# A fused retention and wave-MLP kernel: a new written-out order of its steps, with 39 DMA transposes instead of 35, and output tiles that share the token weights' buffers

## The chip, the core and the metric

The kernel runs on one core of a Trainium2 chip. The metric is the device time of one execution in microseconds; the kernel before has a median of 168.93 us over 11 runs (167.72 to 171.47). Profiles are of single executions.

## What is computed

For 4 batches, 8 heads, 768 tokens and a head width of 64, the state of each head decays by gamma and takes up k times v, and q reads it out:

```python
for t in range(S):
    state = gamma * state + outer(k[t], v[t])      # per batch and head
    y[t] = scale * q[t] @ state
```

The heads' results side by side give x with 512 columns. Then for each batch, with five products of matrices:

```python
theta = x @ w_theta
y = w_tok_r @ (x * cos(theta)) + w_tok_i @ (x * sin(theta))   # over tokens, 768 x 768
u = x + y
out = u + maximum(u @ w_ch, 0)
```

## The kernel before, in words

Both stages are cut into blocks, and the blocks of both are mixed. The retention is cut into 24 *units* n: a batch, a third of its tokens (256) and half of its heads. The MLP is cut into 24 *chunks* C of 128 tokens, six to a batch, and 24 output *tiles* t of 128 tokens, also six to a batch.

For a unit: Lk, Lq and Lv load k, q and v (0.262 MB each). ck, cq and cv cast them to bf16 and scale q and v; the letter after the second point names the engine (p POOL, v DVE, a ACT). k and q have to be transposed: either Tk and Tq do so on PE (4 matmuls each) and E copies the result out of PSUM, or Dk (line 309) does both with one DMA transpose from SBUF to SBUF, issued on SP. G runs three steps on PE: A of this unit (16 matmuls, scores), Y of the unit before (16, scores times v) and ST of this unit (16, the state's increment). m masks the scores on DVE, SU adds up the state on DVE, SB copies it as bf16, I reads the state out with q (2 or 4 matmuls), XA copies the result as xT on ACT.

For a chunk: Hh makes theta (4 matmuls of 512 columns), CN takes sine and cosine on ACT. x itself is xT transposed back, by Tx on PE and a copy Ex, or by Dx (line 434), a DMA transpose on SP. z multiplies x with sine and cosine.

The weights: Lth and Lch load w_theta and w_ch (1.049 MB each), cth and cch cast them. Lw loads a row block of a token weight (0.393 MB; the tile `wtok`, 4 buffers), cw casts it, Tw transposes it on PE (6 matmuls), Ew copies it out.

For a tile: M.t.0 to M.t.5 sum over the six chunks of the batch (2 matmuls of 512 columns each), u adds x on DVE, then u is transposed, by Tu on PE and a copy Eu, or by Du (line 510), a DMA transpose on SP. O multiplies with w_ch (4 matmuls), f (line 519) makes the output tile on DVE, SO stores it from SP or ACT. The last tile is done in halves (Mh, uh, Tuh, Euh, Oh, fh, SOh). warm.n is n matmuls on zeros at the start.

Nothing schedules this but a list: `ORDER` (line 23) names every step, the loop at its end calls them in that order, and each engine and each queue takes its own instructions in that order. An engine whose next instruction waits holds back all that stand behind it. This holds for SP too, which issues all loads, all DMA transposes and most stores. Loads may stand far ahead of their use: k, q and v have 9 buffers each.

```python
    def Dk(n):
        kqT = work.tile([P, 2, 2, 2, P], BF, name="kqT", bufs=4)
        nc.sync.dma_start_transpose(
            out=kqT.rearrange("p w a j t -> p (w a j) t"),
            in_=st["kqb", n].rearrange("p w d -> p (w d)"))
        st["kqT", n] = kqT
```

Of the kernel before, what the change touches and what calls it, by code (L numbers as in the profile page):

```python
# [14 lines left out]
FT = mybir.dt.float32  # L15
# [5 lines left out]


ORDER = """
const1 const2 const4 const3 const7 warm.8 Lk.0.s Lq.0.s ck.0.p Lv.0.s Lk.1.s const6 Lq.1.s Lv.1.s
Lk.2.s cv.0.v Lq.2.s ck.1.a cq.0.p Tk.0 warm.4 Tq.0 E.0.v warm.4 G.0 const5 cq.1.v Lv.2.s SU.0
SB.0.1.v Tk.1 SB.0.0.a warm.2 Tq.1 m.0 ck.2.v E.1.a Lk.3.s cv.1.p Lq.3.s warm.2 I.0 cq.2.p warm.4
G.1 XA.0.0 Tk.2 XA.0.1 cv.2.p Lv.3.s m.1 Lk.4.s cq.3.p SU.1 ck.3.p Tq.2 E.2.a SB.1.1.a Lq.4.s
Lth.s SB.1.0.v cv.3.p warm.7 I.1 G.2 Lv.4.s XA.1.0 Tq.3 Tk.3 XA.1.1 m.2 ck.4.a E.3.v warm.2 Tx.1
cth.3.a SU.2 cq.4.p cth.2.p SB.2.0.v SB.2.1.v Lk.5.s warm.2 Tk.4 Tq.4 Ex.1.v Lq.5.s Lw.0.0.s
cth.1.a warm.2 I.2 E.4.v G.3 SU.3 XA.2.1 cth.0.p SB.3.1.a Tx.0 warm.3 Hh.0 SB.3.0.v cv.4.p XA.2.0  # L30
I.3 m.3 cq.5.v CN.0.1 ck.5.p Lv.5.s CN.0.0 cw.0.0.p Ex.0.v Lk.6.s G.4 Tk.5 SU.4 Tq.5 m.4 Lq.6.s
Lw.1.0.s Hh.1 SB.4.0.a SB.4.1.p E.5.v XA.3.1 Tw.0.0 Lv.6.s cv.5.p Lk.7.s Lq.7.s Ew.0.0.v XA.3.0
I.4 CN.1.0 Tx.3 ck.6.a G.5 cq.6.v Tq.6 Lv.7.s Lk.8.s CN.1.1 Lq.8.s z.0.p SU.5 SB.5.1.p Tk.6
cw.1.0.p cv.6.p Lw.0.1.s m.5 Lv.8.s Ex.3.a XA.4.1 Hh.3 XA.4.0 ck.7.p Tx.2 cq.7.p Lk.9.s E.6.v
Lq.9.s Hh.2 Ex.2.v CN.3.0 ck.8.p SB.5.0.a z.1.v Lw.1.1.s Tw.1.0 Lv.9.s Ew.1.0.v CN.3.1 cq.8.p I.5
cv.7.p CN.2.0 z.3.v cv.8.p G.6 XA.5.1 Tk.7 XA.5.0 Hh.5 Lk.10.s Tq.7 Tk.8 CN.2.1 m.6 CN.5.1 Lq.10.s
CN.5.0 SU.6 Hh.4 E.7.v SB.6.1.a Tq.8 SB.6.0.a Tx.4 M.0.0 I.6 cw.0.1.a G.7 z.2.v E.8.v Ex.4.v Tx.5
SU.7 CN.4.1 Lw.0.2.s M.0.1 Ex.5.v ck.9.p CN.4.0 cq.9.p M.0.2 XA.6.0 Tw.0.1 SB.7.1.p XA.6.1
SB.7.0.a Lw.1.2.s m.7 z.4.v Tk.9 M.0.3 Tq.9 Ew.0.1.a cw.1.1.p I.7 Lv.10.s Lk.11.s G.8 XA.7.0
Lq.11.s z.5.v E.9.a cv.9.p Tw.1.1 M.0.4 Ew.1.1.v XA.7.1 Lw.0.3.s M.0.5 u.0 Lw.1.3.s SU.8 SB.8.0.v  # L40
Hh.6 ck.10.p cq.10.p cw.0.2.p m.8 Lw.0.4.s cw.1.2.p Tk.10 Lw.1.4.s M.1.0 Lv.11.s M.1.1 CN.6.0
cw.0.3.p M.1.2 M.1.3 Tq.10 SB.8.1.a I.8 M.1.4 Tw.0.2 M.1.5 E.10.v Lch.s cw.1.3.p Lk.12.s Lq.12.s
Ew.0.2.v Tw.1.2 CN.6.1 cv.11.p G.9 Ew.1.2.a ck.11.a Hh.7 u.1 M.2.0 ck.12.p XA.8.0 CN.7.0 CN.7.1
M.2.1 cq.11.v cq.12.p cv.10.v SU.9 Lv.12.s Lk.13.s Tk.11 XA.8.1 SB.9.1.v M.2.2 Tq.11 cv.12.p M.2.3
M.2.4 SB.9.0.v ck.13.p Tw.0.3 Dx.6 Lw.0.5.s Lw.1.5.s m.9 M.2.5 Dk.12 E.11.a Tw.1.3 I.9 Lq.13.s
Lv.13.s cw.0.5.p Ew.0.3.v G.10 Lk.14.s Lq.14.s Ew.1.3.a Tu.0 u.2 SU.10 Eu.0.v M.3.0 M.3.1
SB.10.0.a Tu.1 cw.0.4.a cw.1.4.v Lv.14.s Lk.15.s Eu.1.v SB.10.1.v M.3.2 XA.9.0 m.10 M.3.3 cch.3.v
Tx.7 XA.9.1 cq.13.p M.3.4 Ex.7.a M.3.5 Tw.1.4 I.10 Tw.0.4 cch.1.a cch.0.a Dk.13 G.11 Ew.1.4.v
cch.2.v u.3 Tu.2 O.0 SU.11 Ew.0.4.a ck.14.p Tu.3 cv.14.p XA.10.0 M.4.0 Eu.2.a m.11 M.4.1 f.0
Eu.3.v z.6.v M.4.2 M.4.3 Lq.15.s SB.11.0.a O.1 M.4.4 cq.14.p XA.10.1 SB.11.1.a M.4.5 Tw.0.5 f.1  # L50
Lv.15.s Tx.8 Hh.8 Lk.16.s cw.1.5.a Ew.0.5.v I.11 Tw.1.5 u.4 Ex.8.a G.12 Ew.1.5.v Tx.9 M.5.0
Lq.16.s cq.15.p SU.12 M.5.1 z.7.v Ex.9.v Dk.14 CN.8.1 CN.8.0 XA.11.1 Hh.9 SB.12.1.v CN.9.0 Lv.16.s
ck.16.p O.2 XA.11.0 CN.9.1 z.8.v M.5.2 f.2 Lk.17.s M.5.3 Tx.11 M.5.4 Lq.17.s Lv.17.s SB.12.0.a
SO.0.s Ex.11.a M.5.5 Tx.10 Lk.18.s Hh.10 SO.1.s Hh.11 z.9.v cv.13.v SO.2.s Lq.18.s CN.10.0 ck.15.p
Lv.18.s u.5 M.6.0 m.12 M.6.1 CN.10.1 M.6.2 cv.15.p CN.11.1 cq.16.p Ex.10.v I.12 G.13 CN.11.0 M.6.3
z.10.v Tu.5 XA.12.1 z.11.v Eu.5.a M.6.4 SU.13 M.6.5 SB.13.0.v O.3 u.6 Tu.4 M.7.0 ck.17.p M.7.1
M.7.2 Dk.16 M.7.3 M.7.4 SB.13.1.a f.3 M.7.5 m.13 Tk.15 Tq.15 XA.12.0 Eu.4.a Lk.19.s E.15.a I.13
u.7 Lq.19.s G.14 XA.13.0 M.8.0 m.14 SU.14 Lv.19.s XA.13.1 M.8.1 SB.14.0.v M.8.2 SB.14.1.a M.8.3
O.4 M.8.4 M.8.5 f.4 cq.17.p Tu.7 cv.16.p u.8 O.5 f.5 I.14 G.15 m.15 XA.14.1 Dk.17 M.9.0 SU.15
M.9.1 M.9.2 M.9.3 Eu.7.a M.9.4 ck.18.v Dx.13 M.9.5 XA.14.0 SB.15.1.p Hh.13 SB.15.0.p I.15 CN.13.1  # L60
cq.19.p cv.18.v G.16 Lk.20.s u.9 Hh.12 cq.18.p Lq.20.s SU.16 SB.16.0.p XA.15.0 SB.16.1.a M.10.0
XA.15.1 m.16 Du.8 M.10.1 Tu.6 SO.3.s Dx.14 CN.12.0 cq.20.p Lv.20.s CN.12.1 ck.19.v M.10.2 M.10.3
SO.4.s cv.17.v CN.13.0 z.13.p Eu.6.a I.16 cv.20.p G.17 Dk.19 O.7 SU.17 f.7 Tx.12 SB.17.0.a Tq.18
Tk.18 Dx.15 M.10.4 XA.16.1 Ex.12.a Lk.21.s O.6 z.12.p XA.16.0 SB.17.1.v ck.20.a M.10.5 cv.19.v f.6
m.17 SO.5.s u.10 I.17 Hh.15 E.18.a O.8 Du.9 G.18 XA.17.0 f.8 Dx.16 SU.18 ck.21.p Dk.20 Lq.21.s
M.11.0 m.18 M.11.1 CN.15.1 CN.15.0 cq.21.p M.11.2 Hh.14 Lv.21.s M.11.3 SB.18.0.a XA.17.1 Du.10
M.11.4 SB.18.1.a Lk.22.s Lq.22.s cq.22.p z.15.v ck.22.p I.18 M.11.5 SO.7.s CN.14.0 G.19 CN.14.1
Hh.16 u.11 Tx.17 Dk.21 M.12.0 XA.18.0 SU.19 CN.16.0 z.14.v M.12.1 SB.19.0.a Du.11 Hh.17 M.12.2
M.12.3 Lv.22.s Ex.17.v CN.16.1 XA.18.1 CN.17.0 m.19 SB.19.1.a z.16.v CN.17.1 O.9 I.19 SO.6.s G.20
M.12.4 z.17.v M.12.5 f.9 Lk.23.s XA.19.1 Hh.19 Lq.23.s Dk.22 O.10 SU.20 Lv.23.s cv.22.p u.12  # L70
M.14.0 SB.20.0.a m.20 M.14.1 CN.19.0 ck.23.p M.14.2 SB.20.1.v M.14.3 M.14.4 XA.19.0 cv.21.v
cq.23.p M.14.5 I.20 f.10 G.21 O.11 u.14 M.16.0 M.16.1 SU.21 M.16.2 Dx.18 XA.20.1 SB.21.0.a cv.23.p
XA.20.0 M.16.3 M.16.4 M.16.5 SB.21.1.v f.11 CN.19.1 m.21 Hh.18 I.21 u.16 Dk.23 M.15.0 M.15.1 Dx.19
Du.12 CN.18.1 SO.9.a G.22 M.15.2 SU.22 XA.21.0 SB.22.0.v XA.21.1 m.22 M.15.3 M.15.4 Du.16 SO.8.s
M.15.5 CN.18.0 Dx.20 Hh.21 u.15 SB.22.1.p I.22 G.23 XA.22.1 z.18.v M.13.0 z.19.p M.13.1 SU.23 m.23
SO.10.a Hh.20 XA.22.0 SB.23.0.v Dx.21 M.13.2 Du.14 M.13.3 M.13.4 M.20.0 CN.20.1 M.20.1 CN.20.0
CN.21.1 SB.23.1.v O.16 I.23 G.24 XA.23.0 f.16 M.13.5 XA.23.1 CN.21.0 z.20.p O.12 Hh.23 M.22.0 f.12
Hh.22 M.22.1 Dx.22 z.21.p CN.23.0 u.13 Dx.23 M.18.0 CN.22.0 SO.11.s M.22.2 CN.22.1 Du.15 M.18.1
M.20.2 z.22.v M.22.3 CN.23.1 M.18.2 M.18.3 M.22.4 z.23.v O.14 M.20.3 M.22.5 f.14 M.18.4 M.18.5
Du.13 M.20.4 u.22 u.18 M.19.0 O.15 M.17.0 M.19.1 SO.16.a M.17.1 f.15 SO.14.s M.19.2 Du.22 M.19.3  # L80
# [19 lines left out]
def kernel(  # L100
# [14 lines left out]
    B, H, S, D = q.shape  # L115
    dm = H * D
    P = 128
# [10 lines left out]
    io = ctx.enter_context(tc.tile_pool(name="io", bufs=2))  # L128
    work = ctx.enter_context(tc.tile_pool(name="work", bufs=3))
# [131 lines left out]
    st = {}  # L261
# [255 lines left out]
        st["o", t] = o_ps  # L517

    def f(t):
        st["ot", t] = work.tile([P, dm], FT, name="ot", bufs=4)  # L520
        nc.vector.scalar_tensor_tensor(st["ot", t], st["o", t], 0.0, st["u", t], ALU.max,  # L521
                                       ALU.add)

# [86 lines left out]
```

## Time and profile before

| | us |
|---|---|
| median of 11 runs | 168.93 |
| the profiled execution's own time | 169.3 |
| its span, from first to last instruction | 167.6 |
| PE busy in the span | 155.4 |
| DVE busy | 122.4 |
| ACT busy, POOL busy | 79.0, 78.5 |

The loads bring 25.69 MB from HBM, the stores 6.29 MB. TensorE's granted clock is 0.999 of full speed. Busy PE time is modelled and holds overlaps, so work on PE is better counted by the distance from one matmul's start to the next one's. A row of the chain of waits has the start, the duration and the instruction with its line; "SPq" is the issuing queue of SP. In the stretches each engine has its busy time and its number of instructions. The groups by tile give the shortest, median and longest duration in ns.

### The profile page before, as it was taken

To read this page: it belongs to the slowest core of one execution; us is meant where nothing else is said; L and a number is where in the kernel's file an instruction comes from. 1 tells how busy PE (TensorE), PEld (TensorE's weight loads), DVE (VectorE), ACT (ScalarE), POOL (GpSimd) and SP (SyncE) were. 2 spreads that over 40 slices of the span, in tenths; PEclk is the share of its full clock that TensorE was granted. 3 is DMA by queue.
4 is the path that set the end of the run, shared out by engine and by line. 5 is a ranking of instruction groups with operands and counts; after the bars stand their busy time and mean duration, and the time that the engine had idled before them with its cause. 6 is when DMAs were issued, how large, how long until landed. Compare 5 with 4: busy or idle time off the path is not lost.

```text
span 167.6 us, 4924 instructions
## 1 busy us (share of the span) xinstructions
PE 155.4 (93%) x2017; PEld 88.0 (52%) x2044; DVE 122.4 (73%) x200; ACT 79.0 (47%) x159; POOL 78.5 (47%) x99
## 2 busy tenths in 40 slices
PE   7988994999999999999999999999997999999991
PEld 2445563666566746455555555554554444444660
DVE  3397999989898996999669889678745443626552
ACT  5335485896576854655313776662341553000030
POOL 3768477999852643559206395033362380000000
PEclk9999999999999999999999999999999999999999
DMA  5999999999799999999999677799996866336555
GB/s 143 288 290 327 333 322 290 316 322 342 257 286 329 216 232 292 152 290 307 337 217 197 172 195 201 137 276 145 237 223 124 204 86 188 99 89 203 81 189 188
DMA packets 68582, 38.20 MB, mean 228 GB/s; under 512 B 25936, under 2 KB 63056, under 8 KB 68560
## 3 DMA queue, kind: packets, MB, share of 16 engines
q1 hardware_dynamic: 67408, 35.92, 90.4%
q10 hardware_dynamic: 1152, 1.97, 3.5%
q8 instruction: 16, 0.26, 0.7%
q14 instruction: 6, 0.05, 0.1%
HBM read 25.69 MB, written 6.29 MB: 191 GB/s over the span
## 4 chain that ended last, share of the span: by engine, by line
PE 59%; SPq 12%; DMA 10%; POOL 6%; DVE 5%; issue 3%; ACT 1%; DVEq 0%; POOLq 0%
PE y_ps L488 28%; SPq L157 10%; PE o_ps L515 10%; PE th_ps L441 8%; DMA qf<-in_q_dram 7%; DMA kqT<-kqb 3%; POOL kqb L279 2%; PE at_ps L323 2%; POOL vb L285 2%; PE r_ps L393 2%; PE y_ps L538 2%; DVE kqb L279 2%; PE w_ps L472 2%; PE kq_ps L293 1%; PE r_ps L380 1%
## 5 line engine op out<-in xcount | busy, mean ns | idle before, releaser
L488 PE MATMUL y_ps<-z,wtr 128*128 128x512 bf16 x135 | 51.2, 379 | 0.5
L488 PE MATMUL y_ps<-z,wti 128*128 128x512 bf16 x129 | 48.9, 379 | 0.4 <-issue 0.3
L413 ACT CAST xT<-r_ps 128x256 bf16<-128x256 f32 x48 | 16.9, 372 | 31.2 <-PE r_ps L351 20.1
L332 DVE TENSOR_TENSOR at<-at_ps,mask 128x1024 bf16<-128x1024 f32 x24 | 29.1, 1213 | 1.1 <-PE at_ps L323 1.0
L279 POOL TENSOR_TENSOR kqb<-qf,qsc 128x512 bf16<-128x512 f32 x20 | 22.1, 1109 | 14.5 <-DMA qf<-in_q_dram 12.7
L521 DVE SCALAR_TENSOR_TENSOR ot<-o_ps,u 128x512 f32<-128x512 f32 x23 | 15.8, 688 | 15.0 <-PE o_ps L515 14.5
L285 POOL TENSOR_TENSOR vb<-vf,vsc 128x512 bf16<-128x512 f32 x17 | 19.5, 1151 | 11.3 <-DMA vf<-in_v_dram 11.2
L441 PE MATMUL th_ps<-wth,xT 128*128 128x512 bf16 x89 | 23.8, 379 | 0.6 <-POOL wth L139 0.2
L515 PE MATMUL o_ps<-wch,uT 128*128 128x512 bf16 x88 | 23.2, 379 | 0.3
L488 PEld LDWEIGHTS <-wtr 128*128 128x128 bf16 x138 | 13.5, 98 | 13.0
L488 PEld LDWEIGHTS <-wti 128*128 128x128 bf16 x138 | 13.5, 98 | 12.9 <-issue 0.2
L448 ACT ACTIVATE cs<-th_ps,halfpi 128x512 bf16<-128x512 f32 x24 | 16.5, 687 | 7.3 <-PE th_ps L441 5.0
L495 DVE TENSOR_TENSOR u<-y_ps,x_sb 128x512 bf16<-128x512 f32 x23 | 15.8, 685 | 5.6 <-PE y_ps L488 5.6
L448 ACT ACTIVATE cs<-th_ps,zerob 128x512 bf16<-128x512 f32 x24 | 16.2, 686 | 5.4 <-PE th_ps L441 4.4
L455 DVE TENSOR_TENSOR z<-cs,x_sb 128x1024 bf16<-128x1024 bf16 x18 | 14.7, 827 | 3.4 <-ACT cs L448 3.2
L455 POOL TENSOR_TENSOR z<-cs,x_sb 128x1024 bf16<-128x1024 bf16 x6 | 12.7, 2119 | 7.6 <-DMA x_sb<-xT 5.9
L139 POOL CAST kqb<-kf 128x512 bf16<-128x512 f32 x16 | 11.2, 700 | 9.5 <-DMA kf<-in_k_dram 8.1
L258 PE MATMUL y_ps<-zero 128*128 128x512 bf16 x36 | 12.4, 462 | 1.4 <-DVE zero L194 1.3
L441 PEld LDWEIGHTS <-xT 128*128 128x128 bf16 x96 | 8.8, 98 | 9.2 <-issue 0.5
L515 PEld LDWEIGHTS <-uT 128*128 128x128 bf16 x92 | 8.7, 98 | 9.4 <-issue 0.2
L137 ACT COPY uT<-u_ps 128x512 bf16<-128x512 bf16 x6 | 3.5, 589 | 21.2 <-PE u_ps L500 21.2
L293 PE MATMUL kq_ps<-ident,kqb 128*128 128x128 bf16 x112 | 10.0, 223 | 2.6 <-DVE kqb L279 2.3
(74 smaller groups left out, 209.3 us busy)
## 6 DMA issues: line engine op xcount, KB each, us to landing
kf<-in_k_dram SPq DMA_DIRECT2D x24, 256.0 KB, 5.6
qf<-in_q_dram SPq DMA_DIRECT2D x24, 256.0 KB, 5.3
vf<-in_v_dram SPq DMA_DIRECT2D x24, 256.0 KB, 5.6
out_dram<-ot SPq DMA_DIRECT2D x16, 256.0 KB, 3.2
wtok<-in_moe_w_tok_r_dram SPq DMA_DIRECT2D x6, 384.0 KB, 5.5
wtok<-in_moe_w_tok_i_dram SPq DMA_DIRECT2D x6, 384.0 KB, 6.1
out_dram<-ot ACTq DMA_DIRECT2D x7, 256.0 KB, 2.1
w<-in_moe_w_theta_dram SPq DMA_DIRECT2D x1, 1024.0 KB, 7.8
```

Of the source, the lines that this page charges most:

```text
L157: queues[e].dma_start(out=t.rearrange("p h a d -> p h (a d)"), in_=src[b, h * HU:(h + 1) * HU, i * 2 * P:(i + 1) * 2 * P, :].rearrange("h ...
L279: engines[e].tensor_mul(in_blocks(kqb_of(n)[:, 1]), by_token(raw["qf", n]), _bcast_last(K["qsc"][:, i, :, h * HU:(h + 1) * HU], D))
L285: engines[e].tensor_mul(in_blocks(vb), by_token(raw["vf", n]), _bcast_last(K["vsc"][:, i, :, h * HU:(h + 1) * HU], D))
L332: nc.vector.tensor_mul(at.rearrange("p g j a t -> p (g j) (a t)"), st["at_ps", n].rearrange("p g j a t -> p (g j) (a t)"), _bcast_mid(K["m ...
L413: nc.scalar.copy(st["xT", 2 * i + c][:, 2 * h:2 * h + 2].rearrange("p j (t a) -> p j t a", a=2), st["R", n + 1][:, c, :2 * P].rearrange("p ...
L441: nc.tensor.matmul(th_ps, st["xT", C][:, j, :], K["wth"][:, j, :], start=(j == 0), stop=(j == 3))
L448: nc.scalar.activation(st["cs", C][:, w, :], st["th_ps", C], AF.Sin, bias=K["zerob" if w else "halfpi"], scale=1.0)
L455: engines[e].tensor_mul(st["z", b][:, c], st["cs", C], _bcast_mid(x_of(C), 2))
L488: nc.tensor.matmul(st["y", t], K["wT"][r][:, s0, t0 * P:(t0 + 1) * P], st["z", b][:, s0, r, :], start=(s0 == 0 and r == 0), stop=(s0 == nT ...
L495: nc.vector.tensor_add(st["u", t], st["y", t], st["x", b][:, t0, :])
L515: nc.tensor.matmul(o_ps, st["uT", t][:, j, :], K["wch"][:, j, :], start=(j == 0), stop=(j == nD - 1))
L521: nc.vector.scalar_tensor_tensor(st["ot", t], st["o", t], 0.0, st["u", t], ALU.max, ALU.add)
```

## The change

`ORDER` is replaced as a whole, and f takes its output tile from another pool for some tiles:

```diff
     def f(t):
-        st["ot", t] = work.tile([P, dm], FT, name="ot", bufs=4)
+        if t >= 4 and (t < 8 or t % 2):
+            st["ot", t] = io.tile([P, S], FT, name="wtok", bufs=4)[:, :dm]
+        else:
+            st["ot", t] = work.tile([P, dm], FT, name="ot", bufs=4)
         nc.vector.scalar_tensor_tensor(st["ot", t], st["o", t], 0.0, st["u", t], ALU.max,
                                        ALU.add)
```

So tiles 4 to 7 and the odd ones from 9 on use the four buffers of `wtok`, 11 in all; the others keep the four buffers of `ot`.

The same steps stand in the new order but for the choice of how and where. By count:

| | before | after |
|---|---|---|
| Dk, Dx, Du (DMA transposes) | 10, 11, 14 | 11, 11, 17 |
| Tk and Tq, Tx, Tu (on PE) | 14, 13, 9 | 13, 13, 6 |
| warm-up matmuls | 40 | 39 |
| ck on POOL, DVE, ACT | 16, 3, 5 | 9, 8, 7 |
| cq on POOL, DVE | 20, 4 | 13, 11 |
| cv on POOL, DVE | 17, 7 | 19, 5 |
| SB on POOL, DVE, ACT | 7, 18, 23 | 17, 11, 20 |
| Ew on DVE, ACT | 8, 4 | 3, 9 |
| z on POOL, DVE | 6, 18 | 8, 16 |
| SO on SP, ACT | 16, 7 | 9, 14 |

The lines of ORDER around units 8 to 11 and around the last loads:

```diff
-CN.5.0 SU.6 Hh.4 E.7.v SB.6.1.a Tq.8 SB.6.0.a Tx.4 M.0.0 I.6 cw.0.1.a G.7 z.2.v E.8.v Ex.4.v Tx.5
...
-cw.0.3.p M.1.2 M.1.3 Tq.10 SB.8.1.a I.8 M.1.4 Tw.0.2 M.1.5 E.10.v Lch.s cw.1.3.p Lk.12.s Lq.12.s
-Ew.0.2.v Tw.1.2 CN.6.1 cv.11.p G.9 Ew.1.2.a ck.11.a Hh.7 u.1 M.2.0 ck.12.p XA.8.0 CN.7.0 CN.7.1
-M.2.1 cq.11.v cq.12.p cv.10.v SU.9 Lv.12.s Lk.13.s Tk.11 XA.8.1 SB.9.1.v M.2.2 Tq.11 cv.12.p M.2.3
-M.2.4 SB.9.0.v ck.13.p Tw.0.3 Dx.6 Lw.0.5.s Lw.1.5.s m.9 M.2.5 Dk.12 E.11.a Tw.1.3 I.9 Lq.13.s
...
-M.12.4 z.17.v M.12.5 f.9 Lk.23.s XA.19.1 Hh.19 Lq.23.s Dk.22 O.10 SU.20 Lv.23.s cv.22.p u.12
...
+Tw.1.0 G.6 Lch.s z.3.v Tk.8 CN.2.1 XA.5.1 cw.1.1.p Tq.8 E.8.v Ew.1.0.a Hh.5 Lw.0.3.s Tx.5 z.2.v
...
+Tw.0.2 m.6 M.0.5 E.7.a Lq.9.s u.0 G.7 Ew.0.2.v cw.1.2.p Lv.9.s cw.0.3.p Tw.1.2 XA.6.0 M.1.0 M.1.1
...
+Dk.9 cch.1.p cch.3.p Lq.11.s u.2 Tx.6 Hh.6 SB.8.1.v Tx.7 cw.0.4.a M.3.0 cw.1.4.v Lv.11.s M.3.1
+M.3.2 ck.11.v M.3.3 cq.10.p Dk.10 Ex.6.a Du.2 SB.8.0.a cch.0.a cv.10.v Lk.12.s M.3.4 CN.6.0 Ex.7.a
+Tw.1.4 cq.11.v Lq.12.s Lv.12.s CN.6.1 Tk.11 M.3.5 Lw.0.5.s I.8 Tq.11 Ew.1.4.a E.11.a G.9 u.3 z.6.p
...
+M.12.5 XA.19.1 SU.20 Dk.21 Hh.19 SO.5.s SB.20.0.p u.12 O.10 SB.20.1.v XA.19.0 M.14.0 f.10 M.14.1
+m.20 cq.22.v M.14.2 Lv.22.s Lk.23.s ck.22.a M.14.3 I.20 M.14.4 M.14.5 O.11 u.14 G.21 Lq.23.s Dk.22
...
```

## The prediction, made before the changed kernel was run

> **What bounds the kernel now.** I read the page's header and slices first, then the chain of waits, then the stretches, then the groups by tile.
>
> ```profile
> span 167.6 us, 4924 instructions
> ...
> PE 155.4 (93%) x2017; PEld 88.0 (52%) x2044; DVE 122.4 (73%) x200; ACT 79.0 (47%) x159; POOL 78.5 (47%) x99
> ...
> PE   7988994999999999999999999999997999999991
> ...
> DMA  5999999999799999999999677799996866336555
> ```
>
> PE is full from slice 8 to slice 39 except for one dip (slice 31). Before that DMA is full and PE is not. The chain of waits gives the price of PE's work and the two waits:
>
> ```profile
> 19.76 6.31 DMA qf<-in_q_dram
> 26.09 2.54 DVE kqb L279
> 28.67 0.62 PE kq_ps L293 x8
> ...
> 43.41 1.73 PE y_ps L488 x8
> ...
> 47.12 0.35 PE at_ps L323 x16
> 47.47 0.22 PE r_ps L393 x16
> ...
> 49.65 0.22 PE kq_ps L293 x4
> ...
> 51.39 0.34 PE w_ps L472 x6
> ...
> 116.65 5.33 DMA qf<-in_q_dram
> 122.05 1.05 POOL kqb L279
> 123.12 4.98 DMA kqT<-kqb
> 128.14 0.42 PE at_ps L323 x16
> ...
> 162.97 0.67 PE o_ps L563 x6
> ```
>
> A 512-column matmul costs 0.216 us (8 in 1.73), a 128-column one 0.056. By the program: 276 M, 96 Hh and 92 O matmuls make 464 x 0.216 = 100.2; 32 half-width ones x 0.109 = 3.5; 276 transposes x 0.056 = 15.5; 80 of I x 0.056 = 4.5; 24 units of A, Y and ST x (0.35 + 0.22 + 0.33, the last read off the start of the next matmul) = 21.6. Together 145.2 us of work. The 40 warm-up matmuls cost 8.6. PE ends at 163.7, 3.9 before the span's end. So PE's idle is 167.6 - 145.2 - 8.6 - 3.9 = 9.9 us. At the row at 28.67 (Tq.6 and Tk.6) 11.5 of work and 8.6 of warm-up lie behind it, so 8.5 of the idle is already there; only about 1.3 comes in the 135 us after. The span is a load-bound start and then PE work end to end.
>
> Two views set the rate of the loads and what a DMA transpose does to them (columns: stretch; busy us of PE, PEld, DVE, ACT, POOL; clock, DMA share, GB/s):
>
> ```profile
> 20.00:44.00 24.00, 20.65 (x383) 13.12 (x386) 22.42 (x37) 17.98 (x39) 21.68 (x25) 1.00 1.09 323
> 44.00:48.00 4.00, 4.00 (x79) 2.68 (x78) 3.48 (x6) 1.87 (x4) 2.88 (x4) 1.00 0.69 210
> 64.00:73.00 9.00, 8.95 (x106) 5.13 (x105) 8.10 (x14) 5.14 (x11) 4.65 (x5) 1.00 1.29 226
> ```
>
> ```profile
> L309 SPq DMA_TRANSPOSE kqT<-kqb x10: 1237/1521/3442, 57.8 to 123.1; - x10
> DMA to landing us min/median/max: 3.3/5.4/6.3
> ```
>
> The loads stream at 323 GB/s and land in their order on SP. From q of unit 6 (6.68 MB into the order, landed at 26.1) any later load lands at 26.1 + (MB - 6.68)/0.323, later where the stream has a hole. (v of unit 11, 14.41 MB: 50.0, plus 4 us x 113/323 = 1.4 for the hole at 44 to 48; the trace has 51.7.)
>
> **The change, part by part.** *PE's own work.* Unit transposes on PE fall from 14 to 13, u transposes from 9 to 6: 8 + 12 = 20 matmuls x 0.056 = -1.1. One warm-up less: -0.2. The listing agrees: PE has 4048 rows against 4090.
>
> *Casts moved between engines.* cq and ck move from POOL to DVE (cq on DVE 4 to 11, ck 3 to 8); 10 SB go to POOL, 5 Ew from DVE to ACT. DVE changes by +7 x 0.69 (its median) + 5 x 0.69 for cq and ck, -2 x 1.09 (cv), -5 x 0.55 (Ew), -7 x 0.41 (SB), -2 x 0.83 (z), -2.1 (one each of E, Eu, cch) = -3.3; with cq at its mean of 1.15, which holds a 2.53 us case beside a POOL instruction, it is 0. ACT gains 5 x 0.80 + 2 x 0.62 - 3 x 0.37 - 1.8 = +2.3, POOL about -0.8. No engine passes 80% of the span, PE hides all of it: 0. If the cover goes, an early cast costs its 0.7 to 1.1 directly, which is reckoned next.
>
> *The order of the loads.* Theta now comes before v of unit 3, w_ch (1.05 MB) before k of unit 9, and the token weights earlier. Counting megabytes: q of unit 8 is at 9.04 MB (before 8.65), q of unit 11 at 15.20 (before 12.58). That is 1.2 and 8.1 us later at 323 GB/s. PE comes to Tq.8 after 15.9 us of work (before 17.8) and to Tq.11 after 35.4 (before 32.3). Tq.8: lands 26.1 + 2.36/0.323 = 33.4, cast on DVE 0.69, so 34.1; PE had 15.9 + 8.4 of work, so its idle there is 9.8. Before had 9.1 at Tq.8. Cost +0.7. Tq.11: the stream has no hole now, as SP no longer waits for a token-weight buffer at 41 to 45; it lands at 52.5 without transposes. But Dk.9 now stands ahead of it on SP. Dk.9 waits for cq.9 on POOL (v of unit 9, 13.37 MB, lands at 46.8; cv.9 then cq.9, 1.1 each: 48.9), and the loads of q and v 11 queue behind it on SP.
>
> What does Dk.9 cost the stream? The trace has transposes among loads in 64 to 73: 226 GB/s instead of 323 is 0.87 MB or 2.7 us lost, and two units' own 0.52 MB are another 1.6: 2.1 us each. The Trainium skill, "Advanced Engine Details and Errata", section "X-Bar Transpose (TRN2)", says that transpose DMAs here are as fast as regular ones; then 0.26 MB costs 0.8. By the rule q 11 lands at 53.3, its cast ends at 54.0, idle 10.2. By the row it is 54.6, 55.3, and PE's work of 35.4 + 8.4 makes the idle 11.5. I take the row, since it is the same transpose among the same loads. Cost over the 9.8: +1.7 (between 0.4 and 1.7; 0 if something earlier has delayed PE). G.9, which needs Dk.9's landing, comes right behind Tq.11 and waits for the same stream; on DVE u.3, SU.9 and m.9 stand behind cq.11, and two of them need G.9 anyway. Next late would be q of unit 12 (15.98 MB, with two Dk and Du.2, taken at 1.0, ahead): 26.1 + 28.8 + 4.2 + 1.0 = 60.1, met after 41.9 of work at about 62. Not late.
>
> *39 transposes instead of 35.* SP: 4 x 1.29 more, 7 stores fewer (x 0.54): +1.4 on a queue with 90 to 100 us of work. Du.2 and Du.3 have 14 and 9.6 us of PE work until O uses them, so the median landing of 3.0 is hidden. The late Dk have less room: from their place to G it is 4.2 to 6.3 us of PE work for units 19 to 23, against 4.6 to 10 before, and landing takes 5.4. SP may run ahead of its place: Dk.21 can go when ck.21 is done on ACT (92.3 of work), then SP needs 1.3 + 0.5 + 3 x 0.6 until q 23: at 95.9 to 96.7. The chain then needs 11.5 (116.65 to 128.14) and G.23 stands at 109.5: 1.3 to spare. In before the same count gives 13.7 of room, SP came 3.1 late, and the wait was 1.1. If SP is 3.1 late here too, 1.8. Between 0 and 1.8 for G.23 and as much again for G.21 and G.22; I take the trace's own later idle, 0.7.
>
> *Output tiles.* Eleven of the 19 tiles from 4 to 22 take the token weights' buffers, free by then; stores move late, 14 on ACT's queue at 0.34 each, on an engine half idle. The tightest reuse is f.22 behind SO.16, 2.6 us of PE work against a landing of 3.2: 0 to 0.6, taken as 0, as DVE has slack there. ACT's stores at 105 stand ahead of XA, 3 x 0.34: hidden.
>
> *Sum.* 144.1 + 8.4 + idle (9.8 + 1.7 + 0.7 = 12.2) + 3.9 = 168.6, against a span of 167.6: +1.0. The profiled execution took 169.3; the median is 168.93. 168.9 + 1.0 = 169.9.
>
> **The rivals.**
> (a) Forecast: load wait at Tq.11; 169.9. Chance 0.38. With SP also late at the last units (+1.1 to +3): up to 172.5. Chance 0.12.
> (b) The wait is small, the transpose cheap as the rule has it: idle 10.2 + 0.7, span 167.3, time 168.6. Chance 0.22.
> (c) The loads win: place Tq.11, price 1.7. If the hole of 44 to 48 in before was only filled, and Dk.9's data movement fits beside the loads, q 11's cast ends before PE arrives at 53.6; this decides at a transpose cost of 0.4 us or less. Then idle stays at 9.5 to 9.8 and, with G.23's wait gone by SP running ahead, the span is 144.1 + 8.4 + 9.6 + 3.9 = 166.0: time 167.3. For it: PE's idle in before hardly grows after 30 us though DMA is full until 55. Against: DMA has no spare in 20 to 44. Chance 0.28.
> (d) That the change does not do what it says is excluded by the row counts.
>
> **How the numbers follow.** A measurement here tells 0.5%, 0.8 us, from no change. (a) is slower: 0.50. (b) is within: 0.22. (c) is faster: 0.28. The range goes from (c) to the late end of (a): 167.0 to 172.4.
>
> **What would show it.** Right: PE idle of about 11.5 when Tq.11 starts, 1 to 2 us of it just before that transpose or before G.9, with DVE's cq.11 waiting for qf; q 8's transpose near 34; a dip in GB/s at about 49 to 55. The saving shows as 104 kq_ps and 24 u_ps transposes. Wrong: PE unbroken from 35 to 60; or idle that arises after 90 us (then SP's queue was the matter); or DVE waiting on stores before f.

## The result, and the profile after

The changed kernel has a median of 171.41 us (12 runs, 170.22 to 173.92). 47 runs of the kernel before have a median of 170.56. The ratio is **1.0147, 95% interval 1.0113 to 1.0181**: slower by about 2.5 us, where 1.0 us had been forecast. Every ratio takes only the executions within 1.5% of the fastest of their kernel (here 11 of the 12 and 18 of the 47), which is why it is larger than the quotient of these medians, and the runs e8_35 and e18_cq8 were profiled in slower executions, so that of these two only the ratios are used. All ratios below are against the kernel before, run in the same series. The profiled execution took 171.45 us with a span of 169.7, so the span grew by 2.1.

The page's header and slices (PE, PE's clock, DMA in 40 slices of 4.24 us):

```profile
span 169.7 us, 4897 instructions
...
PE 155.1 (91%) x1996; PEld 87.6 (52%) x2023; DVE 111.9 (66%) x193; ACT 80.7 (48%) x160; POOL 76.0 (45%) x101
...
PE   7999659878999999997999999999999999999991
...
PEclk9999995999999999999999999999999999999999
DMA  4999999999989899989999694979999568543535
```

PE has 21 matmuls fewer, as forecast (counted by its weight loads, PEld: 2023 against 2044; some matmul rows are missing from a trace). Slices 5 and 6 are now 6 and 5 and slices 8 to 10 are 8, 7 and 8, where before all five were 9 (its only early hole is the 4 in slice 7): most of the loss lies ahead of 42 us. Later there is one dip in each, in slice 19 here and in slice 31 before. In slice 7 the TensorE clock was 5 tenths. DVE's busy time has fallen by 10.5 us, which did not help.

The stretches (columns as in the prediction) show what the stream of loads did:

```profile
20.00:44.00 24.00, 18.95 (x352) 13.05 (x360) 19.12 (x32) 16.51 (x32) 18.70 (x19) 0.93 1.06 325
44.00:48.00 4.00, 3.95 (x69) 2.51 (x58) 3.35 (x7) 2.85 (x6) 2.58 (x4) 1.00 1.12 336
48.00:56.00 8.00, 7.95 (x105) 4.83 (x104) 6.24 (x12) 4.59 (x11) 3.82 (x6) 1.00 0.83 197
```

In 20 to 44 the loads stream at 325 GB/s as before, yet PE, DVE, ACT and POOL are all less busy (PE 18.95 of 24 instead of 20.65). Every engine waits more while the loads run at their old rate. So the rate of the loads is not at fault: either a load stands at a worse place in the order, or the engines wait for each other. The hole at 44 to 48 is filled (336 instead of 210). The dip that was forecast for 49 to 55 came (197 in 48 to 56), but PE was busy through it (7.95 of 8 us).

I use the prediction's measure, PE's idle: the start of a matmul less the work and warm-up ahead of it (a matmul at a lower clock counts as idle here too). Counted through the program from the trace:

| idle, us, at | before | after |
|---|---|---|
| I.3 (unit 3 read out) | 5.9 | 8.1 |
| M.0.0 (first product of the first tile) | 9.1 | 13.0 |
| Tq.11 | 9.3 | 12.8 |
| the last matmul | 9.8 | 13.3 |

Work is 144.1 and warm-up 8.4, as forecast, 1.3 less than before. Idle is 3.5 more. The difference, 2.2, is the 2.1 of the span. All of the 3.5 is there at 36 to 40 us.

PE's rows at the three largest of these waits (start, us, and in brackets the idle before and who ended it):

```profile
20.21 0.38 PE L379 MATMUL r_ps<-kqT,sbd 128*128 128x128 bf16 x4 [1.08 <-DVE sbd L138]
...
24.80 0.38 PE L379 MATMUL r_ps<-kqT,sbd 128*128 128x128 bf16 x4 [1.87 <-DVE sbd L138]
...
38.94 0.60 PE L440 MATMUL th_ps<-wth,xT 128*128 128x512 bf16 x2 [1.67 <-ACT xT L412]
```

(Lines of the new kernel before f are one lower than before.) These are I.2, I.3 and the second half of Hh.4, ahead of Tx.4. None of them waits directly for a load or for the cast of one. The chain of waits from theta's load on says for what the first two wait:

```profile
8.84 7.23 DMA w<-in_moe_w_theta_dram
16.09 1.14 ACT wth L136 x2
17.22 0.28 ACT xT L412
17.53 0.30 DVE s L364
17.86 0.29 DVE s L366
...
20.21 0.38 PE r_ps L379 x4
...
22.30 0.69 ACT cs L447
22.99 0.27 ACT xT L412
23.28 0.30 DVE s L364
23.61 0.29 DVE s L366
23.90 0.76 DVE sbd L138
```

XA (xT, on ACT) and SU (s, on DVE) read the same PSUM tile: r_ps of unit n+1 holds the read-out of unit n, which XA.n copies, and the increment of the state, which SU.(n+1) adds. There is one buffer of it, so the next I waits for both. And the program keeps the two from reading it at once: whichever stands first in the list goes first, and the other waits. The rows show it: s begins at 17.53, after xT has ended (17.50), and XA.1.1 begins at 18.18, after the second s has ended. ACT's rows:

```profile
18.18 0.37 ACT L412 CAST xT<-r_ps 128x256 bf16<-128x256 f32 x1 [0.68 <-DVE s L366]
...
38.51 0.37 ACT L412 CAST xT<-r_ps 128x256 bf16<-128x256 f32 x1 [2.11 <-DVE s L366]
```

The Trainium skill ("PSUM — Partial Sum Buffer", "Terms") states that two engines on the same bank and partitions at once is an error, reads too; no run here tries it. In the new order theta's two casts stand ahead of XA.1.0 on ACT, so SU.2 on DVE waits for theta, which it does not need, and E.3, m.2 and SB.2.0 behind it on DVE come late for I.2. SU.3 waits for XA.2.0, a cosine (CN.1.0) and XA.2.1. At the third place it is the other way round (second row above): SU.6 stands on DVE behind z.3, E.8, z.2 and Ex.5, XA.5.0 on ACT waits for SU.6, and Hh.4 needs XA.5.0.

The waits view, sums over the whole span (us in total, times, longest), of before:

```profile
ACT xT L413 <- DVE s L365: 6.6, 5, 2.0
ACT xT L413 <- DVE s L367: 2.9, 4, 1.0
DVE s L365 <- ACT xT L413: 1.9, 1, 1.9
```

and of after:

```profile
DVE s L364 <- ACT xT L412: 10.5, 9, 2.6
ACT xT L412 <- DVE s L366: 10.2, 7, 3.6
ACT xT L412 <- DVE s L364: 5.0, 3, 2.4
```

These sums on DVE waited 1.9 us for ACT's copies before and wait 10.5 now; the three rows together grew from 11.4 to 25.7 us. (The step that begins a batch's state, on another line, waited 0.8 before and 1.8 now.) In 15 to 45 us it is 2.6 before and 7.5 after. What comes later delays PE little: by the table its idle grows by only 0.3 from M.0.0 to the end (a wait of 1.0 ahead of I.13 is in it).

The DMA transposes, the prediction's main suspect, are cheaper than before. Their group by tile (duration on SP min/median/max in ns, issue to landing in us):

```profile
L308 SPq DMA_TRANSPOSE kqT<-kqb x11: 1232/1237/1343, 48.6 to 123.5; - x11
...
DMA to landing us min/median/max: 3.2/3.7/5.2
```

The median landing took 3.7 instead of 5.4. q of unit 11 landed at 53.28 (forecast 54.6 by the row, 53.3 by the skill's rule), its cast was done at 55.3, and PE came to Tq.11 only at 56.6. There was no wait.

### The profile page after: what moved, and what is told of

Same layout as the page of the kernel before. It is cut to its first block, busy times and chain, and to the rows that moved or that the text cites. A ratio compares the mean times of both kernels' runs of the same rounds, so it can differ in the third digit from the quotient of the medians.

```text
span 169.7 us, 4897 instructions
## 1 busy us (share of the span) xinstructions
PE 155.1 (91%) x1996; PEld 87.6 (52%) x2023; DVE 111.9 (66%) x193; ACT 80.7 (48%) x160; POOL 76.0 (45%) x101
## 4 chain that ended last, share of the span: by engine, by line
PE 69%; DVE 11%; ACT 5%; SPq 4%; DMA 4%; issue 3%; DVEq 0%; ACTq 0%
PE y_ps L487 33%; PE o_ps L514 11%; PE th_ps L440 9%; SPq L156 4%; DMA w<-in_moe_w_theta_dram 4%; PE at_ps L322 4%; DVE z L454 3%; DVE at L331 3%; PE r_ps L392 2%; PE r_ps L379 2%; ACT cs L447 2%; PE w_ps L471 2%; PE y_ps L540 2%; ACT xT L412 1%; DVE kqT L138 1%
## 5 line engine op out<-in xcount | busy, mean ns | idle before, releaser
L487 PE MATMUL y_ps<-z,wti 128*128 128x512 bf16 x127 | 48.1, 379 | 0.5 <-issue 0.5
L412 ACT CAST xT<-r_ps 128x256 bf16<-128x256 f32 x48 | 17.6, 376 | 33.7 <-PE r_ps L350 17.5
L440 PE MATMUL th_ps<-wth,xT 128*128 128x512 bf16 x91 | 24.8, 388 | 2.2 <-ACT xT L412 1.7
L284 POOL TENSOR_TENSOR vb<-vf,vsc 128x512 bf16<-128x512 f32 x19 | 20.6, 1090 | 8.9 <-DMA vf<-in_v_dram 8.8
L454 POOL TENSOR_TENSOR z<-cs,x_sb 128x1024 bf16<-128x1024 bf16 x8 | 17.0, 2128 | 12.9 <-ACT cs L447 7.6
L138 POOL CAST sbd<-s 64x256 bf16<-64x256 f32 (+1 forms) x17 | 6.4, 379 | 29.8 <-DVE s L364 15.7
L278 POOL TENSOR_TENSOR kqb<-qf,qsc 128x512 bf16<-128x512 f32 x13 | 14.0, 1075 | 3.3 <-DMA qf<-in_q_dram 3.1
L440 PEld LDWEIGHTS <-xT 128*128 128x128 bf16 x96 | 9.0, 100 | 11.1 <-ACT xT L412 2.4
L523 DVE SCALAR_TENSOR_TENSOR ot<-o_ps,u 128x512 f32<-128x512 f32 x12 | 8.2, 687 | 7.7 <-PE o_ps L514 7.6
L136 ACT COPY uT<-u_ps 128x512 bf16<-128x512 bf16 x4 | 2.3, 583 | 20.6 <-PE u_ps L499 20.6
L364 DVE TENSOR_TENSOR s<-r_ps,s 128x128 f32<-128x128 f32 x16 | 4.6, 288 | 10.8 <-ACT xT L412 10.5
```

Of the source, the lines that this page charges most:

```text
L278: engines[e].tensor_mul(in_blocks(kqb_of(n)[:, 1]), by_token(raw["qf", n]), _bcast_last(K["qsc"][:, i, :, h * HU:(h + 1) * HU], D))
L284: engines[e].tensor_mul(in_blocks(vb), by_token(raw["vf", n]), _bcast_last(K["vsc"][:, i, :, h * HU:(h + 1) * HU], D))
L412: nc.scalar.copy(st["xT", 2 * i + c][:, 2 * h:2 * h + 2].rearrange("p j (t a) -> p j t a", a=2), st["R", n + 1][:, c, :2 * P].rearrange("p ...
L440: nc.tensor.matmul(th_ps, st["xT", C][:, j, :], K["wth"][:, j, :], start=(j == 0), stop=(j == 3))
L454: engines[e].tensor_mul(st["z", b][:, c], st["cs", C], _bcast_mid(x_of(C), 2))
L487: nc.tensor.matmul(st["y", t], K["wT"][r][:, s0, t0 * P:(t0 + 1) * P], st["z", b][:, s0, r, :], start=(s0 == 0 and r == 0), stop=(s0 == nT ...
```

## The experiments

Two theories stand against each other. The state chain (S): SU, XA and SB hand over between DVE and ACT in the order of the list, and PE waits for it at the start. The loads (L): theta, w_ch and the token weights, now earlier, delay the units' loads and casts. A third is the DMA transposes themselves (in the expectations of e1 and e2, theory R: SP's queue, transposes and output buffers). Some runs join two orders; a join adds waits of its own.

**Halves of the order.** e1_bstart takes the order of before up to u.0 and the new one for what remains; e2_astart the reverse.

```diff
 e1:  before's order ... u.0 | the remaining steps as the new order has them
 e2:  new order ... u.0      | the remaining steps as the order of before has them
```

> The list of before up to its step u.0 (about 41 us), then the new list for all steps that are left; 38 DMA transposes, 144.6 us of PE work. Theory S (the loss lies in the new start, where PE waits for the state's chain over ACT and DVE): the start's idle falls from 13.0 to about 9.4, the rest costs as in the new kernel: span about 166.8, 0.8 us faster than before, ratio 0.995. Theory R (the loss lies in the rest: SP's queue, transposes, output buffers): slower than before by about 2 us, ratio 1.012. Theory L (the prediction's: q of unit 11 late behind w_ch and Dk.9): as S, since the loads up to that of q 11 now come in the old order.

> The new list up to its step u.0 (about 43 us), then the old list for the rest; 35 DMA transposes, 145.2 us of PE work, output tiles as before. Theory S: the start's idle of 13.0 stays, and the saved transposes are gone: span about 171, 3.4 us slower than before, ratio 1.02. Theory R: as before, ratio 1.00. Theory L: about 1 us slower or less, ratio 1.005, as w_ch stays early but Dk.9 is gone.

Measured: 1.0325 (1.0247 to 1.0402) and 1.0379 (1.0274 to 1.0485). Both are slower than either whole order. Just behind the join, in e1, PE waited 0.8 at M.0.5 for z.5 on DVE, and 2.0 at Tw.1.3 for a row block of token weights that the new order would have loaded long before; in e2 it waited 2.2 at Tq.9, for the cast of a q that the old order loads late. The start of e2 has the waits of after, and that of e1 has not, but the times settle nothing. Inconclusive.

**SU moved forward alone.** e3_su23 puts SU.2 ahead of XA.1.0 and SU.3 ahead of XA.2.0; e4_su6 puts SU.6 ahead of z.3; e5_su236 does both. No load, cast or engine changes.

```diff
-... XA.1.0 SU.2 Tq.3 ...   -... XA.2.0 Lq.5.s CN.1.0 XA.2.1 SU.3 cv.4.p ...
+... SU.2 XA.1.0 Tq.3 ...   +... SU.3 XA.2.0 Lq.5.s CN.1.0 XA.2.1 cv.4.p ...
-... Lch.s z.3.v ... z.2.v Ex.5.v SU.6 XA.5.0 Hh.4 Tx.4 ...
+... Lch.s SU.6 z.3.v ... z.2.v Ex.5.v XA.5.0 Hh.4 Tx.4 ...
```

> The new kernel with two steps moved: SU.2 ahead of XA.1.0 and SU.3 ahead of XA.2.0, so DVE's state sums no longer stand behind ACT's copies of the same PSUM tile (and behind the theta casts and CN.1.0 on ACT). Theory S: PE's waits before I.2 (1.1 us) and I.3 (1.9 us) go, about 1.5 us stays gained after the next limit (the casts of unit 5); 1.5 us faster than the new kernel, ratio to before about 1.006. Theory L: no change against the new kernel, ratio to before 1.015.

> The new kernel with one step moved: SU.6 ahead of z.3 on DVE, in place of behind z.3, E.8, z.2 and Ex.5. Theory S: XA.5.0 comes about 2 us earlier, PE's wait of 1.7 us in Hh.4 goes; about 1.5 us faster than the new kernel, ratio to before about 1.006. Theory L: no change against the new kernel, ratio to before 1.015.

> The new kernel with SU.2, SU.3 and SU.6 all moved ahead (the two edits before this, together). Theory S (only the state's chain over ACT and DVE limits the start): idle at M.0.0 falls from 13.0 to about 9.5, 3 us faster than the new kernel, ratio to before 0.997. Theory S+L (two limits one behind the other: behind the chain stands the row block w_tok_r 3, which lands late as w_ch is ahead of it): idle is about 10 at M.0.0 but 12.0 at Tw.0.3, so only 1 us faster than the new kernel, ratio 1.008.

Measured: e3 1.0118 (1.0044 to 1.0191), e4 1.0091 (1.0056 to 1.0127), e5 1.0053 (1.0019 to 1.0086). Of these intervals only e5's lies clear of the new order's (1.0113 to 1.0181). In e3 the wait at I.2 fell from 1.08 to 0.28 and the one at I.3 from 1.87 to 1.50; in e4 the one within Hh.4 fell from 1.67 to 0.35; in e5 idle at M.0.0 was 11.1 instead of 13.0. Three steps moved forward in the list gave back about 0.9 of the 1.5%: the state chain is the larger part. New waits of 0.5 and 0.8 appeared (Tw.0.3 in e3; ahead of Tw.0.2 in e5), so the gain is less than the sum of the waits removed.

**Loads moved back.** e6_lch puts the load of w_ch behind k of unit 11; e7_su_lch does so on top of e5.

```diff
-... G.6 Lch.s z.3.v ...  M.1.2 ck.9.a cch.2.v Tu.0 ...  Lk.11.s XA.7.1 Dk.9 ...  cch.0.a cv.10.v ...
+... G.6 z.3.v ...        M.1.2 ck.9.a Tu.0 ...  Lk.11.s Lch.s XA.7.1 Dk.9 ...  cch.0.a cch.2.v cv.10.v ...
```

> The new kernel with the load of w_ch moved from ahead of k 9 to behind k 11 (its cast on DVE moved back with it); the chain of the start untouched. Theory S+L: alone it gains nothing, as PE has already lost 13 us of idle at 40 us, when the loads are in time: ratio to before as the new kernel's, 1.012 to 1.015. Theory L alone (the loads are the limit all through): 1.5 us faster, ratio 1.006.

> Both edits: the three SU ahead and w_ch loaded later. Theory S+L: both limits gone, idle about 10 at M.0.0 and 10.5 at Tw.0.3: 2.5 us faster than the new kernel, ratio to before about 1.000. Theory S alone: the same as with the three SU alone.

Measured: 1.0233 (1.0145 to 1.0322) and 1.0257 (1.0194 to 1.0319). e7 is slower than e5; e6's interval overlaps the new order's. Idle at M.0.0 fell to 11.7 and 10.9, but Tq.11 then waited 2.53 and 2.64. The edit also puts a cast of w_ch (cch.2) ahead of cq.11 on DVE. In e6 this cast took 2.38 us beside POOL's z.6, and cq.11 began only at 57.17. In e7 cq.11 began at 54.58 and took 2.60 us beside z.6 (54.08, 2.56 us); in after, with z.6 at 55.47, it took 0.68. So the wait moved to the place that the prediction had named, for casts on DVE and not for a load, and what a later w_ch is worth without that stays unknown.

**35 DMA transposes in the new order.** e8_35 does Dk.9, Du.2, Du.3 and Du.6 on PE again.

```diff
-... XA.7.1 Dk.9 ...          ... Du.2 ... Du.3 ... Du.6 ...
+... XA.7.1 Tq.9 Tk.9 E.9.v ...   ... Tu.2 Eu.2.a ... Tu.3 Eu.3.a ... Tu.6 Eu.6.a ...
```

> The new kernel with four DMA transposes done on PE instead (unit 9 by Tq, Tk and E on DVE, tiles 2, 3 and 6 by Tu and Eu on ACT): 35 transposes, 20 matmuls or 1.1 us more on PE. If the four transposes cost nothing on SP and the DMA engines: 1.1 us slower than the new kernel, ratio to before about 1.020. If they cost what they save (prediction: 1.7 us at Tq.11): no change or 0.6 us faster, ratio 1.010 to 1.014.

Measured: 1.0364 (1.0297 to 1.0431), 2.1% above the new order, where the added PE work is 1.1 us (0.6%). So doing them on PE at the same places does not help, and nothing here says that the four more DMA transposes make the new order slow. Where the other 1.5% arises is not known: on PE the replaced steps can wait as well, and there is no profile of this run to tell.

**The reverse: before with one part of the change, or with its fault.** e9_bf changes only f. e10_before_su6 writes the fault into the order of before at one place.

```diff
 e10, in the order of before:
-... XA.5.1 Tk.7 XA.5.0 Hh.5 ... CN.5.0 SU.6 Hh.4 E.7.v ... G.7 z.2.v E.8.v ...
+... XA.5.1 Tk.7 Hh.5 ... CN.5.0 E.7.v z.2.v SU.6 XA.5.0 Hh.4 ... G.7 E.8.v ...
```

> The kernel before with nothing changed but f: the output tiles 4 to 7 and the odd ones from 9 on in the token weights' buffers. All theories (state chain, loads): ratio 1.000, within 0.3%; PE idle at the end 9.8 us as before. If the ratio is over 1.004, the buffers and not the order are part of the cause.

> The kernel before with the fault of the new order written in at one place: E.7.v and z.2.v stand ahead of SU.6, and XA.5.0 stands behind SU.6, so the state sum waits behind two DVE steps and xT behind the sum. No load moves and no work is added. State-chain theory: SU.6 slips from 33.9 to about 35.9, XA.5.0 from 32.8 to about 36.5, and PE waits about 2.4 us ahead of Hh.4 at 34.6; up to 1.1 of it is given back at G.23, so the span grows by 1.3 to 2.4 us and the ratio is 1.008 to 1.014. Load theory: PE's start is set by when k, q, v and the weights land, which is unchanged, so the ratio is 1.000 to 1.003.

Measured: e9 0.9994 (0.9954 to 1.0033): no cost of the output tiles' buffers shows. e10 1.0184 (1.0095 to 1.0273), span 168.8, idle at the end 11.1 instead of 9.8. ACT's timeline of e10:

```profile
36.99 0.37 ACT L413 CAST xT<-r_ps 128x256 bf16<-128x256 f32 x1 [1.42 <-DVE s L367]
```

And PE's, at Hh.4:

```profile
37.41 0.61 PE L441 MATMUL th_ps<-wth,xT 128*128 128x512 bf16 x2 [1.65 <-ACT xT L413]
```

With no load moved, three steps moved in the list make the kernel before slower by at least 0.95%. The loads' 1.000 to 1.003 is excluded; the wait was 1.65 instead of 2.4 us.

**Before, with less waiting.** e11_before_z0 puts z.0 on DVE, because Tq.6 in before waited 2.3 us for a cq.6 that took 2.53 us beside POOL's z.0. e12_before_z0_du adds Du.2, Du.3, Du.6.

```diff
-... z.0.p ...                     -... u.3 Tu.2 O.0 ... Eu.2.a ...
+... z.0.v ...   (e11 and e12)     +... u.3 Du.2 O.0 ...   (e12; 3 and 6 likewise)
```

> The kernel before with z.0 on DVE instead of POOL. In before, cq.6 on DVE took 2.53 us beside POOL's z.0, and Tq.6 waited 2.2 us for it. If the two steps slowed each other, cq.6 takes 0.7 us and Tq.6 starts up to 1.9 us earlier; z.0 itself adds about 0.8 us on DVE. Span 0.5 to 1.9 us shorter, ratio 0.989 to 0.997. If the loads hold PE's start anyway, the wait moves to the next load-fed step and the ratio is 0.998 to 1.001.

> The kernel before with z.0 on DVE and with Du.2, Du.3, Du.6 in place of Tu and Eu of these tiles, so 38 DMA transposes. If a late DMA transpose of u is free, 12 matmuls of 0.056 us are saved on top of the run with z.0 alone: 0.7 us less, ratio 0.004 lower than that run. If each costs the stream of loads its time, the ratio is the same as or above that run.

Measured: e11 0.9983 (0.9929 to 1.0037). cq.6 took 0.67 us, Tq.6 began at 27.5 instead of 28.7, and idle at the end was 8.5 in the profiled execution; the timed runs cannot tell this from no change. e12 1.0267 (1.0212 to 1.0323), a miss. PE's timeline of e12:

```profile
71.08 0.60 PE L515 MATMUL o_ps<-wch,uT 128*128 128x512 bf16 x2 [3.41 <-DMA uT<-u]
```

O.2 waited for Du.2. SP came to it only at 66.04, behind Dk.13, and it landed at 71.03. Whether these DMA transposes were free depended on where SP stood: in the new order SP came to Du.2 at 52.85, and it landed at 55.58, in time.

**What was left of e5's 0.5%.** e13_su_sb3 puts SB.3.1 ahead of XA.2.0 on ACT; e14_su_v3 loads and casts v of unit 3 ahead of theta; e15_su_sb3_v3 does both. All stand on e5.

```diff
 e13:  -SU.3 XA.2.0 Lq.5.s CN.1.0 XA.2.1 cv.4.p SB.3.1.a   +SU.3 SB.3.1.a XA.2.0 Lq.5.s CN.1.0 XA.2.1 cv.4.p
 e14:  -Lth.s ... Lv.3.s ... cth.1.p ... cv.3.p            +Lv.3.s Lth.s ... cv.3.p cth.1.p
```

> The run with the three state sums moved forward, and SB.3.1 (the second bf16 copy of unit 3's state, on ACT) ahead of XA.2.0, CN.1.0 and XA.2.1. In that run I.3 still waited 1.75 us, ended by this copy at 23.58. State-chain theory: the copy runs at about 22.3, I.3 at about 22.9, PE's idle at the end falls from 12.3 by 0.5 to 1.1, ratio 1.000 to 1.003. Load theory: the next load-fed step takes the wait, ratio 1.005 as in that run.

> The run with the three state sums moved forward, and v of unit 3 loaded ahead of theta and cast ahead of theta's casts, as in the kernel before. Load theory: theta ahead of v of unit 3 was a cost by itself; v lands at 15.4 instead of 18.1, G.3 is no longer held by its cast at 19.2, and idle falls by 0.5 to 1: ratio 1.000 to 1.003. State-chain theory: G.3 stands behind I.2, which waits for SB.2, and theta's casts then end 0.8 us later on ACT: ratio 1.004 to 1.008.

> Both edits. If they are independent, the gains add: idle at the end 10.5 to 11.5, span 167 to 168, ratio 0.996 to 1.001, so that the whole cost of the new order lies in its start. If a wait at 36 to 46 us takes them back (weight rows behind the other loads), idle stays at 12 and the ratio at 1.003 to 1.006.

Measured: 1.0053 (1.0024 to 1.0082), 1.0118 (1.0021 to 1.0215), 1.0092 (1.0053 to 1.0131). v ahead of theta does not help: in e14 theta's casts on ACT ended only at 19.34, XA.1.0 stood behind them, and Tx.0 waited 2.38 for it instead of 0.52. In e13 the start got shorter (idle 10.7 at M.0.0 against 11.1), and 1.58 came at Tq.11. DVE's timeline of e13:

```profile
53.76 2.30 DVE L279 TENSOR_TENSOR kqb<-qf,qsc 128x512 bf16<-128x512 f32 x1 [0.84 <-DMA qf<-in_q_dram]
```

and POOL's:

```profile
53.39 2.12 POOL L455 TENSOR_TENSOR z<-cs,x_sb 128x1024 bf16<-128x1024 bf16 x1 [2.60 <-ACT cs L448]
```

The cast met z.6, as in e7: 2.30 us for a cast of 0.68.

**The list without these faults.** e16_cq11 is e13 with cq.11 on POOL, ahead of z.6. e17_cq11_su also puts SU.4 ahead of XA.3.1 and SU.13 ahead of XA.12.0. e18_cq8 moves cq.8, which waits for a load, behind SU.6.

```diff
-... Tw.1.4 cq.11.v ...   -... XA.3.1 Lk.6.s Tq.5 SU.4 ...   -... XA.12.0 ... XA.12.1 SU.13 ...
+... Tw.1.4 cq.11.p ...   +... SU.4 XA.3.1 Lk.6.s Tq.5 ...   +... SU.13 XA.12.0 ... XA.12.1 ...
 e18:  -cq.8.v CN.2.0 ... G.6 Lch.s SU.6 z.3.v     +CN.2.0 ... G.6 Lch.s SU.6 cq.8.v z.3.v
```

> The run with SU.2, SU.3, SU.6 and SB.3.1 moved forward, and the cast of q of unit 11 on POOL instead of DVE. In that run the start was shorter (idle 10.7 at 55 us against 12.9 in the new order) but Tq.11 then waited 1.58 us, for a cast that took 2.30 us on DVE beside POOL's z.6. State-chain theory, with the collision as the second cause: cast at 53.7 to 54.8 on POOL, Tq.11 at about 54.9, idle 12.85 falls by 1.1 to 1.4, span about 168.0, ratio 0.996 to 1.000. Load theory: q of unit 11 lands late anyway and something else behind it waits, ratio 1.004 to 1.006.

> As the run before it, with SU.4 ahead of XA.3.1 and SU.13 ahead of XA.12.0 besides. In the new order DVE's SU.13 waits for XA.12.1 on ACT and z.11 behind it takes 1.66 us beside a POOL cast; PE waits 1.0 for it ahead of I.13. State-chain theory: the 1.0 at I.13 goes, and some of the 0.5 to 0.8 at 25 to 27 us: idle 1.0 to 1.5 less, ratio 0.988 to 0.994, faster than both kernels. If the waits only move, ratio as in the run before it.

> As the run before it, with cq.8 on DVE behind SU.6 instead of ahead of it. In that run cq.8 waited on DVE for q of unit 8 (landed 33.4), SU.6 ran behind it at 34.11 and xT on ACT at 34.87 behind that; PE waited 0.71 ahead of Hh.5 and 0.66 ahead of Tx.5. State-chain theory: SU.6 at about 32.8, the two waits fall by 0.7 to 1.3 together, span 165.7 to 166.3, ratio 0.991 to 0.995: faster than both kernels. Load theory (Tk.8 and Tq.8 wait for k and q of unit 8 by 1.1 us, and that is now the limit): ratio 0.997 to 1.000.

Measured: e16 1.0053 (1.0020 to 1.0086), e17 **0.9987 (0.9956 to 1.0018)**, e18 0.9965 (0.9928 to 1.0002). e16's profiled execution did what was expected (Tq.11's wait gone, idle at the end 11.7, span 168.1), its timed ratio did not move from e13's. e17's interval lies clear of e16's, and SU.4 and SU.13 are all that differs. In e17 the 1.0 us that after loses ahead of I.13 is gone too, idle at the end is 10.6 and the span 167.0. The waits view of e17:

```profile
ACT xT L413 <- DVE s L367: 8.5, 7, 2.2
DVE s L365 <- ACT xT L413: 5.8, 6, 2.5
ACT xT L413 <- DVE s L365: 4.5, 3, 2.2
```

(18.8 us together instead of 25.7), and its chain of waits around the read of unit 8:

```profile
28.21 5.19 DMA qf<-in_q_dram
...
33.50 0.06 DVE kqb L279
...
34.11 0.29 DVE s L363
...
34.49 0.29 DVE s L367
34.79 1.12 DVE z L455
```

Now the chain reaches back to a load again: q of unit 8, then its cast, then the state sum behind it on DVE. e18 takes the sum out of that row. It is the best version found, and its interval still touches 1: with 39 DMA transposes and the weights early, the order is as fast as before, not shown to be faster.

In size theory S promised too much: 0.997 for e5, 0.996 to 1.000 for e16, 0.988 to 0.994 for e17. Each wait that was removed let another one show.

## Why the prediction was right in direction and wrong in cause

*The direction and the saving.* PE's work and warm-up fell to 144.1 and 8.4, as counted. The tail was as taken. Slower was right, but by luck: the term that made the forecast slower, Tq.11's +1.7, did not arise, and a cost that had been put at 0 took its place. Idle of 12.2 had been summed and 13.3 was measured: 3.2 too little at the start, 1.7 too much at Tq.11, and 0.4 too much elsewhere.

*The step that failed* is "Casts moved between engines ... PE hides all of it: 0". It held the engines' totals against the span and took the start as bound by loads and early casts alone. It moved steps by count and never asked what each waits for in its new place. The order of ACT's and DVE's steps on one PSUM tile was not looked at. e3 to e5, e13 and e17 move only such steps (and, from e16 on, one cast, which by itself changed no ratio): from 1.0147 to 0.9987, the whole loss. e10 writes the same fault into before and makes it slower. Idle at M.0.0 came to 13.0, where the prediction had 9.8 at Tq.8 just before. The totals themselves were off too: DVE's fell by 10.5 (forecast 0 to 3.3), ACT's rose by 1.7 (2.3), POOL's fell by 2.5 (0.8).

*Tq.8, +0.7.* Right as a floor, hidden in after by larger waits. In e17, where they are gone, Tq.8 begins at 34.25, forecast 34.1, and waits for its cast.

*Tq.11, +1.7.* Did not arise: the early idle had delayed PE, the case that the prediction had put at 0. Two terms were also mis-sized. k of unit 11 landed at 50.6, where 323 GB/s gave 51.7. And q behind Dk.9 landed 2.65 later in after, 1.89 in e17 (50.77 to 52.66). Less the 0.81 of its own load, Dk.9 cost 1.8 and 1.1: between the row's 2.1 and the 0.8 that the Trainium skill's rule ("Advanced Engine Details and Errata", "X-Bar Transpose (TRN2)") gives. Both hold SP's time as well as the stream's: in after SP issued Dk.9 at 48.64, when its casts were done, and q only at 50.05, and q landed 3.2 after that. So the trace does not decide between the row and the rule. That 53.28 equals the rule's number comes from both errors together. In e6, e7 and e13 Tq.11 does wait, but for slow casts. (In e13 cq.11 began 0.84 late for its load as well; with a cast of 0.68 it would, by estimate, have ended at 54.4, and PE came at 54.5.)

*Late stage, +0.7.* After has +0.5 from Tq.11 to the end, as before has. Its cause was not SP's queue: idle grows by 1.0 ahead of I.13, which e17 removes by SU.13 ahead of XA.12.0, and falls a little later, where work costs less than its count. G.21 to G.23 did not wait.

*Output tiles, 0.* Within e9's interval.

*Rivals.* (b) priced the transpose as the rule does, (c) let the loads win. Neither had a wait between engines at the start, and such a wait is what decided. Of the listed signs only the dip in GB/s came; "DVE's cq.11 waiting for qf" and "1 to 2 us just before that transpose" were absent, q 8's transpose stood at 35.2, and idle at Tq.11 was 12.8. Of the listed signs of error none fits either, since PE was broken at 38 us.

*Still open.* What the half clock in slice 7 costs was not separated; in the times it does not show: the two executions of after with a mean clock of 0.99 took 171.42 and 171.45 us, the nine others in the ratio, with 1.00, have a median of 171.29. e16 and e11 show gains of 1.1 and 1.3 us in the span of the profiled execution that the timed runs do not show. Loads that stand at a worse place were tested only with casts moved as well (e6, e7, e14).

## What to carry to other kernels

When a written-out order changes, follow each tile that two engines read: the one listed first holds the other, and whatever that one waits for (here theta's cast, a cosine, a load) is waited for twice. Totals of busy time and of bytes did not show it here; the waits view does, as the sum of waits of each of two engines for the other. Put the step that feeds the next unit's state ahead of the copy that feeds a later stage, and look at which steps of DVE and POOL will coincide.

## What the runs showed of the hardware

*TensorE's clock.* After PE had 1.9 us of idle ahead of I.3 the granted clock fell. Two stretches of after:

```profile
22.00:25.00 3.00, 1.13 (x18) 0.89 (x15) 1.91 (x5) 2.32 (x5) 3.00 (x4) 1.00 1.07 334
27.00:30.00 3.00, 2.78 (x27) 2.03 (x30) 3.00 (x4) 1.82 (x5) 2.02 (x3) 0.55 1.04 276
```

In 22 to 25 PE was busy 1.13 of 3 us; in 27 to 30 it ran at 0.55. In before a stretch of 26 to 30 with 1.69 of 4 us busy and a wait of 2.26 left the clock at 1.00. e5 and e13 have the drop too (in slice 7), after waits of 1.48 and 1.33 at I.3; e3 has none after 1.50. So the length of one wait does not decide it in these runs. The Trainium skill ("TensorE: Matmul & The Clock Gate", "What's actually happening") names an idle window of about 3.4 us; here the longest wait ahead of the drop was 1.9, with low use around it.

*DVE beside POOL.* A cast of q (128x512 from f32) on DVE took mostly 0.67 to 0.69 us, and 2.30 to 2.60 when it began just after POOL's z had begun (before, e7, e13). Each time it ended 0.55 us after z: in the lines of e13, z ends at 55.51 and the cast at 56.06. So the two did not share the time; the cast lasted as if it had run only when z was over. PE then waited 1.4 to 2.5 us at the next transpose. In e3 the cast began 0.59 ahead of z and took 0.69.
